# Splitting value products by the contraction, and issuing query turns ahead of stores, in an attention-then-FFN kernel

## Chip, cores, metric

One core of a Trainium2 chip. The metric is device time in microseconds (us), lower is better; it is the span of the profile plus about 2.0 us.

## The reference, cut to what matters

```python
kv  = einsum('bhsd,bhse->bhde', k, v)      # batch 8, 8 heads, 576 rows, 64 columns
out = einsum('bhsd,bhde->bhse', q, kv)
x   = rmsnorm(out) * g_norm                # then (8*576, 512), normed again with rms_g
y   = (silu(x @ w_gate) * (x @ w_val)) @ w_out   # 512 -> 1536 -> 512
```

## The kernel before

TensorE does everything in bfloat16. Batch 0 is the start-up: its x, its weights and its first products are made while the loads arrive. The weights are rounded and scaled by other engines as they land (`round_w`); the contraction of 512 is four slices `s` of 128. First place that the change touches, the products of the first two pairs of hidden blocks on the first half of the tokens, and the turns (transposes by TensorE) of the second half of x:

```python
for blk, s in ((0, 0), (0, 1), (1, 0), (0, 2), (1, 1), (1, 2)):
    round_w(blk, "v", s, GP)                    # GpSimd rounds value weights
# ... gate products of pairs 0 and 1 ...
for blk in range(2):
    round_w(blk, "v", 3, SC)                    # ScalarE rounds the fourth slices
for u in range(2):
    ffn.half_unit(first[1], u, wv_sb, u, 0, 256)       # all four slices of one block
for u in range(2):
    x_turn(Z, u, xs[u], DVE)                           # turn on TensorE, copy on VectorE
for u in range(2):
    ffn.half_unit(second[1], u, wv_sb, 2 + u, 0, 256)
# next: products that need both turned tiles of x
```

Between the two places, batch 1's q is turned as soon as it is loaded and cast:

```python
down_part(0, 2, 4)
turns.q_turn(0, SC)          # first set of eight turns
down_part(1, 2, 4)
turns.q_turn(1, DVE)         # second set
for c in range(2, 4):
    down_part(c, 2, 4)
# then F: the query products of batch 1
```

Second place, the end of batch 0. `down_out` copies an output bank and, after every second one, stores it; `q_rows` lets the transfer engines turn batch 2's queries. Loads, stores and these turns all go through one queue in program order:

```python
alloc_q(2)
cast_q(2, 0, SC)
ffn.down_out(0)
down_part(1, 8, 12)
f_x(0, xs[0], SC); f_x(1, xs[1], SC)       # (two lines in the kernel)
for i in (1, 2, 3):
    cast_q(2, i, SC if i == 1 else DVE)
ffn.down_out(1)                            # first stores
atts = {b: Att(b) for b in range(2, B + 1)}
for c in range(2):
    atts[2].q_rows(c)
# ...
for c in range(2, 4):
    atts[2].q_rows(c)
ffn.down_out(2)
ffn.down_out(3)                            # second stores
```

Of the kernel before, what the change touches and what calls it, by code (L numbers as in the profile page):

```python
# [20 lines left out]
def kernel(  # L21
# [14 lines left out]
    B, H, S, D = q.shape  # L36
# [5 lines left out]
    T = 4  # L42
    MAIN = 128 * T
    TAIL = S - MAIN
    NS = d_model // 128
# [30 lines left out]
    PE, DVE, SC, GP = nc.tensor, nc.vector, nc.scalar, nc.gpsimd  # L76
# [15 lines left out]
    wv_sb = consts.tile([128, NS, d_ff], BF16, name="wv_sb")  # L92
# [47 lines left out]
    def alloc_q(b):  # L140
        bufs[b]["q"] = qb_pool.tile([128, T, H, D], BF16, name="qb")

    def cast_heads(b, h, n, step, engine):

        src = raws[b, "q"].rearrange("p (h t d) -> p t h d", h=H, t=T)
        at = place(h)
        cast(
            engine, bufs[b]["q"][:, :, at : at + (n - 1) * step + 1 : step, :],
            src[:, :, h : h + (n - 1) * step + 1 : step, :],
        )  # L150

    def cast_q(b, i, engine):

        cast_heads(b, i, 2, 4, engine)
# [29 lines left out]
    def round_w(blk, name, s, engine):  # L184
        j0, j1 = W_BLOCKS[blk]
        dst = {"g": wg_sb, "v": wv_sb}[name][:, s, j0 * 128 : j1 * 128]
        src = w_st[name, blk][:, s, :]
        if engine is SC:
            SC.activation(out=dst, in_=src, func=ACT.Copy, scale=rowscale[:, s : s + 1])
        else:  # L190
            engine.tensor_scalar(  # L191
                out=dst, in0=src, scalar1=rowscale[:, s : s + 1], scalar2=1.0, op0=OP.mult, op1=OP.mult
            )
# [49 lines left out]
    xnts = {}  # L243
# [15 lines left out]
    def to_rows(x, n, c, ps, engine):  # L259

        for j in range(NS):
            PE.matmul(  # L262
                ps[:, j, :], lhsT=x[:, 2 * j : 2 * j + 2, :], rhs=identity, is_transpose=True,
                start=(j == 0), stop=(j == NS - 1),
            )
        cast(engine, xnts[n][:, :, 128 * c : 128 * c + 128], ps)
# [198 lines left out]
    class Ffn:  # L465
# [25 lines left out]
        def half_unit(self, ps, u, wt, j, lo, hi):  # L491

            for s in range(NS):
# [2 lines left out]
                    rhs=xnts[self.n][:, s, lo:hi], start=(s == 0), stop=(s == NS - 1),  # L496
                )

        def up_pair(self, i, lo, banks=None):

            banks = banks or self.pair_banks()
            for k, wt in enumerate((wg_sb, wv_sb)):
                for u in range(2):
                    self.half_unit(banks[k], u, wt, 2 * i + u, lo, lo + 256)
            return banks
# [123 lines left out]
    Z = Cols(0, 256, 512, qt0, sqt0, "Z")  # L629
# [44 lines left out]
    def x_turn(cols, c, x, engine, p=att_pool, name="att_ps"):  # L674
        bank = p.tile([128, MAIN], FP32, name=name)
        to_rows(x, cols.n, cols.lo // 128 + c, bank.bitcast(BF16)[:, 0:512].rearrange("p (j t) -> p j t", j=NS), engine)
# [70 lines left out]
    xs = [A.scale(c, oA[c]) for c in range(2)]  # L747
# [4 lines left out]
        x_turn(A, i, xs[i], DVE, *((ops_pool, "o_ps") if i else ()))  # L752
    round_w(1, "g", 2, DVE)
    round_w(1, "g", 3, SC)
    for blk, s in ((0, 0), (0, 1), (1, 0), (0, 2), (1, 1), (1, 2)):
        round_w(blk, "v", s, GP)
    ffn = Ffn(0)
    first, second = ffn.pair_banks(), ffn.pair_banks()
# [12 lines left out]
        round_w(blk, "v", 3, SC)  # L771
    SC.preload_act_table(ACT.Silu)
    xs = [Z.scale(c, oZ[c]) for c in range(2)]
    for u in range(2):
        ffn.half_unit(first[1], u, wv_sb, u, 0, 256)
    for u in range(2):
        x_turn(Z, u, xs[u], DVE)
    for u in range(2):
        ffn.half_unit(second[1], u, wv_sb, 2 + u, 0, 256)
    ffn.gate_pair(0, 0, first)  # L780
    ffn.gate_pair(1, 0, second)
    for name in ("g", "v"):
# [102 lines left out]
    def f_x(c, x, engine):  # L885
        bank = att_pool.tile([128, NS, 128], BF16, name="att_ps")
        to_rows(x, 1, c, bank, engine)
# [3 lines left out]
    def down_part(c, lo, hi):  # L891
        ffn.down_products(c, lo, hi, pools[c])
# [39 lines left out]
    down_part(0, 8, 12)  # L932
    xs = [F.scale(c, F.outa[c]) for c in range(4)]
    alloc_q(2)
    cast_q(2, 0, SC)
    ffn.down_out(0)
    down_part(1, 8, 12)
    f_x(0, xs[0], SC)
    f_x(1, xs[1], SC)
    for i in (1, 2, 3):  # L940
        cast_q(2, i, SC if i == 1 else DVE)
    ffn.down_out(1)
    atts = {b: Att(b) for b in range(2, B + 1)}
    for c in range(2):
        atts[2].q_rows(c)
    down_part(2, 8, 12)
    f_x(2, xs[2], DVE)
    f_x(3, xs[3], DVE)
    down_part(3, 8, 12)
    for c in range(2, 4):  # L950
        atts[2].q_rows(c)
    ffn.down_out(2)
    ffn.down_out(3)



# [28 lines left out]
    for n in range(1, B + 1):  # L985
        ffn = Ffn(n)
# [11 lines left out]
        if n < B:  # L998
# [5 lines left out]
            for i in range(2):  # L1004
                u = o0 + 2 * i
# [9 lines left out]
        b = n + 2  # L1015
# [53 lines left out]
```

## Time and profile before

| | |
|---|---|
| time, first three runs | 319.75 us median (319.25 to 320.18) |
| span of the profiled run | 318.0 us |
| TensorE busy | 97% |
| its wait for GpSimd's rounding, near 20 us | 0.63 us |
| its wait for batch 2's query turns, near 65 us | 0.54 us by the distance of the neighbours' starts |

How to read it: TensorE is the bound, so a change is worth what it takes out of TensorE's idle gaps, and only if no later gate swallows it. The lines are shown in the prediction.

### The profile page before, as it was taken

What the parts mean: (1) busy time and instruction counts of PE and PEld (TensorE: products, weight loads), DVE (VectorE), ACT (ScalarE), POOL (GpSimd) and SP (SyncE); (2) the same over time, 40 slices, a digit from 0 to 9 for tenths busy, and PEclk for the clock granted to TensorE, in tenths of its full rate; (3) what the DMA queues carried; (4) which work ended last, traced back from release to release, by engine and by line L of the source; (5) the groups of instructions that cost most, each with busy time, mean ns of one, the idle gap of its engine ahead of it and who ended that gap; (6) DMA issues with size and microseconds to landing.
All of it is one profiled execution on the core that took longest, in us unless ns stands there. A gap on an engine that the chain in (4) does not pass through costs nothing.

```text
span 318.0 us, 5995 instructions
## 1 busy us (share of the span) xinstructions
PE 308.1 (97%) x2334; PEld 150.3 (47%) x2371; DVE 180.4 (57%) x378; ACT 175.7 (55%) x323; POOL 21.4 (7%) x46
## 2 busy tenths in 40 slices
PE   7899999999999999999999999999999999999995
PEld 3575456444444444444444444444444444444443
DVE  3676768679439922893289427951795079604310
ACT  3577367475657466836683768366745374233321
POOL 1274351100000000000000000000000000000000
PEclk9999999999999999999999999999999999999999
DMA  7999999886379257905790499838002710230014
GB/s 264 361 386 388 376 375 332 136 237 259 75 193 354 77 135 195 364 8 96 195 378 27 89 194 232 316 66 174 28 0 58 142 66 3 56 142 3 0 33 100
DMA packets 60712, 54.95 MB, mean 173 GB/s; under 512 B 36232, under 2 KB 45708, under 8 KB 60684
## 3 DMA queue, kind: packets, MB, share of 16 engines
q1 hardware_dynamic: 60304, 53.92, 57.5%
q10 hardware_dynamic: 380, 0.66, 0.6%
q8 instruction: 18, 0.29, 0.4%
q14 instruction: 10, 0.08, 0.1%
HBM read 37.75 MB, written 9.44 MB: 148 GB/s over the span
## 4 chain that ended last, share of the span: by engine, by line
PE 90%; DMA 5%; SPq 1%; issue 1%; another core or an unknown queue 1%; POOL 1%; ACT 0%; DVE 0%
PE v_ps L477 28%; PE g_ps L477 28%; PE o_ps L519 26%; DMA st<-in_moe_w_val_dram 3%; DMA st<-in_q_dram 2%; PE att_ps L286 2%; PE v_ps L519 1%; PE g_ps L519 1%; PE v_ps L494 1%; DMA out_dram<-o_sb 1%; PE att_ps L326 1%; POOL wv_sb L191 1%; PE o_ps L494 1%; PE att_ps L262 0%
## 5 line engine op out<-in xcount | busy, mean ns | idle before, releaser
L483 DVE TENSOR_TENSOR h_sb<-silu,v_ps 128x512 bf16<-128x512 bf16 x104 | 71.1, 683 | 100.8 <-ACT silu L482 68.1
L477 PE MATMUL v_ps<-xnt,wv_sb 128*128 128x512 bf16 x409 | 106.2, 379 | 0.7
L477 PE MATMUL g_ps<-xnt,wg_sb 128*128 128x512 bf16 x398 | 104.6, 379 | 0.7
L482 ACT ACTIVATE silu<-g_ps 128x512 bf16<-128x512 f32 x104 | 62.1, 597 | 70.7 <-PE g_ps L477 55.0
L519 PE MATMUL o_ps<-wo_sb,h_sb 128*128 128x512 bf16 x386 | 86.8, 379 | 0.4
L477 PEld LDWEIGHTS <-wv_sb 128*128 128x128 bf16 x416 | 40.7, 98 | 49.1
L519 PEld LDWEIGHTS <-h_sb 128*128 128x128 bf16 x420 | 40.6, 98 | 47.7 <-issue 0.4
L477 PEld LDWEIGHTS <-wg_sb 128*128 128x128 bf16 x416 | 39.6, 98 | 46.4
L104 ACT COPY o_sb<-o_ps 128x512 f32<-128x512 f32 (+1 forms) x34 | 19.7, 579 | 40.2 <-PE o_ps L519 36.6
L373 DVE TENSOR_TENSOR xna<-outa,s1y 128x512 bf16<-128x512 bf16 x28 | 17.9, 684 | 0.0
L104 ACT CAST vb<-st 128x576 bf16<-128x576 f32 x25 | 15.7, 673 | 3.7 <-DMA st<-in_v_dram 3.7
L104 ACT CAST qb<-st 128x512 bf16<-128x512 f32 (+1 forms) x30 | 16.3, 602 | 2.1 <-DMA st<-in_q_dram 2.1
L356 DVE TENSOR_REDUCE ssq<-sq 128x16 f32<-128x1024 bf16 x14 | 17.1, 1220 | 0.5
L356 DVE TENSOR_REDUCE ssq<-sqt 128x16 f32<-128x1024 bf16 x14 | 17.1, 1220 | 0.5
L104 ACT CAST kb<-st 128x576 bf16<-128x576 f32 x20 | 12.4, 674 | 0.0
L341 ACT ACTIVATE sq<-att_ps 128x512 bf16<-128x512 f32 x14 | 7.6, 594 | 4.3 <-PE att_ps L326 3.6
L619 PE MATMUL att_ps<-kv_all 128*128 128x512 bf16 (+1 forms) x21 | 7.6, 489 | 1.2 <-DVE sel L608 1.2
L355 DVE TENSOR_TENSOR sq<-sq,gsq 128x512 bf16<-128x512 bf16 x14 | 5.9, 421 | 4.9 <-ACT sq L341 4.9
L106 DVE CAST kb<-st 128x576 bf16<-128x576 f32 x12 | 5.9, 508 | 4.0 <-DMA st<-in_k_dram 4.0
L106 POOL CAST wo_sb<-st 128x512 bf16<-128x512 f32 x12 | 7.2, 632 | 7.4 <-DMA st<-in_moe_w_out_dram 7.4
L341 ACT ACTIVATE sqt<-o_ps 128x512 bf16<-128x512 f32 x14 | 7.6, 598 | 0.0
L347 ACT CAST outa<-att_ps 128x512 bf16<-128x512 f32 x14 | 7.5, 594 | 0.0
(148 smaller groups left out, 180.6 us busy)
## 6 DMA issues: line engine op xcount, KB each, us to landing
st<-in_k_dram SPq DMA_DIRECT2D x7, 1152.0 KB, 10.8
st<-in_v_dram SPq DMA_DIRECT2D x7, 1152.0 KB, 12.6
out_dram<-o_sb SPq DMA_DIRECT2D x14, 512.0 KB, 3.1
st<-in_q_dram SPq DMA_DIRECT2D x6, 1024.0 KB, 8.0
st<-in_moe_w_out_dram SPq DMA_DIRECT2D x6, 512.0 KB, 10.4
st<-in_moe_w_gate_dram SPq DMA_DIRECT2D x4, 512.0 KB, 10.6
st<-in_moe_w_val_dram SPq DMA_DIRECT2D x4, 512.0 KB, 9.9
st<-in_k_dram SPq DMA_DIRECT2D x4, 288.0 KB, 4.4
```

The lines of the kernel that those rows point to most:

```text
L104: engine.copy(out=dst, in_=src)
L106: engine.tensor_copy(out=dst, in_=src)
L286: PE.matmul(self.kv_ps[x][to, a, :], lhsT=kb[rows, 2 * a + x, c, :], rhs=vb[rows, 2 * a + x, c, :], start=(a == 0 and c == 0), stop=(a == ...
L341: SC.activation(out=self.in_place(self.sq[i][:, 0], g), in_=bank, func=ACT.Square)
L347: SC.copy(out=self.in_place(rows, g), in_=bank)
L356: DVE.reduce_sum(out=self.ssq[:, c], in_=sq, axis=AX.X)
L373: DVE.tensor_tensor(out=self.xna[c], in0=self.outa[c], in1=self.alpha[:, c, :].to_broadcast([128, H, D]), op=OP.mult)
L477: PE.matmul(ps, lhsT=wt[:, s, j * 128 : (j + 1) * 128], rhs=x[:, s, :], start=(s == 0), stop=(s == NS - 1),)
L482: SC.activation(out=silu, in_=g_ps, func=ACT.Silu)
L483: DVE.tensor_tensor(out=self.h[:, j, :], in0=silu, in1=v_ps, op=OP.mult)
L519: PE.matmul(self.o_ps[c], lhsT=self.h[:, j, c * 128 : (c + 1) * 128], rhs=wo_sb[:, j, :], start=(j == 0), stop=(j == NF - 1),)
L619: PE.matmul(ps[:, 0:w], lhsT=warm_sb[:, 0:128], rhs=warm_sb[:, 0:w], start=True, stop=True, skip_group_check=True)
```

## The change

Its intent: fill the wait for rounding with slices that are ready and with the turns of x; and issue the queries' turns before the stores, so that they land before TensorE wants them. No work is added or removed. Two stretches are cut where they are marked.

```diff
+        def half_units(self, ps, wt, j, lo, ss):
+            for u in range(2):
+                for s in ss:
+                    PE.matmul(
+                        ps[:, u, :], lhsT=wt[:, s, (j + u) * 128 : (j + u + 1) * 128],
+                        rhs=xnts[self.n][:, s, lo : lo + 256],
+                        start=(u == 0 and s == 0), stop=(u == 1 and s == NS - 1), skip_group_check=True,
+                    )
@@ part 1 @@
-    for blk, s in ((0, 0), (0, 1), (1, 0), (0, 2), (1, 1), (1, 2)):
+    for blk, s in ((0, 0), (0, 1), (1, 0), (1, 1), (0, 2), (1, 2)):
         round_w(blk, "v", s, GP)
... cut ...
-    for u in range(2):
-        ffn.half_unit(first[1], u, wv_sb, u, 0, 256)
-    for u in range(2):
-        x_turn(Z, u, xs[u], DVE)
-    for u in range(2):
-        ffn.half_unit(second[1], u, wv_sb, 2 + u, 0, 256)
+    ffn.half_units(first[1], wv_sb, 0, 0, (0, 1))
+    ffn.half_units(second[1], wv_sb, 2, 0, (0, 1))
+    x_turn(Z, 0, xs[0], DVE)
+    ffn.half_units(first[1], wv_sb, 0, 0, (2, 3))
+    x_turn(Z, 1, xs[1], DVE)
+    ffn.half_units(second[1], wv_sb, 2, 0, (2, 3))
@@ part 2 @@
-    cast_q(2, 0, SC)
-    ffn.down_out(0)
+    for i in range(T):
+        cast_q(2, i, SC if i < 2 else DVE)
+    atts = {b: Att(b) for b in range(2, B + 1)}
+    for c in range(T):
+        atts[2].q_rows(c)
     down_part(1, 8, 12)
     f_x(0, xs[0], SC)
     f_x(1, xs[1], SC)
... cut: the old casts, turns and stores between and behind the other parts go ...
     down_part(3, 8, 12)
-    for c in range(2, 4):
-        atts[2].q_rows(c)
-    ffn.down_out(2)
-    ffn.down_out(3)
+    for c in range(T):
+        ffn.down_out(c)
```

More of the change, by code (lines that the diff above doesn't have):

```diff
@@ L939 @@
     f_x(1, xs[1], SC)
-    for i in (1, 2, 3):
-        cast_q(2, i, SC if i == 1 else DVE)
-    ffn.down_out(1)
-    atts = {b: Att(b) for b in range(2, B + 1)}
-    for c in range(2):
-        atts[2].q_rows(c)
     down_part(2, 8, 12)
@@ L949 @@
     down_part(3, 8, 12)
-    for c in range(2, 4):
-        atts[2].q_rows(c)
-    ffn.down_out(2)
-    ffn.down_out(3)
+    for c in range(T):
+        ffn.down_out(c)
     def load_q_tails():
```

## The prediction

> **What bounds the kernel now.** I read the page first, then the list of TensorE's waits, then the timeline around each wait, because the change moves only a few dozen instructions and its worth is decided by individual gaps.
>
> ```profile
> PE 308.1 (97%) x2334; PEld 150.3 (47%) x2371; DVE 180.4 (57%) x378; ACT 175.7 (55%) x323; POOL 21.4 (7%) x46
> ```
>
> TensorE is busy 97% of a 318.0 us span, the others at most 57%. No work of TensorE is removed, so only its idle gaps can be won. From TensorE's list of waits, the two that the change is aimed at (us in total, times, longest):
>
> ```profile
> PE v_ps L494 <- POOL wv_sb L191: 0.6, 1, 0.6
> PE o_ps L326 <- DMA qt<-qb: 0.4, 1, 0.4
> ```
>
> The first: the value products of the first pair stand at the third slice of the contraction, because GpSimd has not rounded that slice of the weights yet. TensorE's timeline there (start, duration), then GpSimd's:
>
> ```profile
> 20.50 0.83 PE L494 MATMUL v_ps<-xnt,wv_sb 128*128 128x256 bf16 x6 [0.63 <-POOL wv_sb L191]
> 21.16 0.61 PE L262 MATMUL att_ps<-identity,xna 128*128 128x128 bf16 x8
> 21.61 1.04 PE L494 MATMUL v_ps<-xnt,wv_sb 128*128 128x256 bf16 x8
> 22.48 1.04 PE L494 MATMUL o_ps<-xnt,wg_sb 128*128 128x256 bf16 x8
> ```
> ```profile
> 18.60 2.75 POOL L191 TENSOR_SCALAR wv_sb<-st,rowscale 128x256 bf16<-128x256 f32 x6 [1.00 <-DMA st<-in_moe_w_val_dram]
> ```
>
> A 256-column matmul costs (22.48 - 21.61)/8 = 0.109 us start to start, a turn (21.61 - 21.16)/8 = 0.056 us, a rounding 2.75/6 = 0.46 us. The wait ends at 20.50, just after the fourth rounding (18.60 + 4 x 0.46 = 20.44).
>
> The second gap is larger than the list says. TensorE from the value products of a unit to those of the next, with batch 2's query products between them, and below it the same place one batch later:
>
> ```profile
> 63.73 1.03 PE L477 MATMUL v_ps<-xnt,wv_sb 128*128 128x512 bf16 x4
> ...
> 66.67 1.03 PE L477 MATMUL v_ps<-xnt,wv_sb 128*128 128x512 bf16 x4
> ```
> ```profile
> 93.39 1.03 PE L477 MATMUL v_ps<-xnt,wv_sb 128*128 128x512 bf16 x4
> ...
> 95.79 1.03 PE L477 MATMUL v_ps<-xnt,wv_sb 128*128 128x512 bf16 x4
> ```
>
> Same work: 2.94 us against 2.40, so this wait costs 0.54 us. Its cause is the order of the transfer queue:
>
> ```profile
> 55.04 1.26 SPq L539 DMA_DIRECT2D out_dram<-o_sb  x2
> 56.40 6.10 SPq L300 DMA_TRANSPOSE qt<-qb  x4
> 62.61 1.92 SPq L539 DMA_DIRECT2D out_dram<-o_sb  x2
> ```
>
> The four query turns stand behind the first two stores. The first is issued at 56.40, the last at 61.2 with up to 4.3 us to landing (all four: 2.5 to 4.3), near 65.5, when the query products resume (65.58).
>
> Between the two gaps lies a third place, which the change doesn't touch: batch 1's second half of q. VectorE casts it when the load lands, and TensorE turns it:
>
> ```profile
> 42.40 0.63 DVE L106 CAST qb<-st 128x512 bf16<-128x512 f32 x2 [0.72 <-DMA st<-in_q_dram]
> ```
> ```profile
> 42.79 0.83 PE L833 MATMUL g_ps<-identity,qb 128*128 128x128 bf16 x8
> 43.67 0.38 PE L519 MATMUL o_ps<-wo_sb,h_sb 128*128 128x512 bf16 x1
> 43.88 0.61 PE L833 MATMUL v_ps<-identity,qb 128*128 128x128 bf16 x8
> 44.33 0.59 PE L519 MATMUL g_ps<-wo_sb,h_sb 128*128 128x512 bf16 x2
> ```
>
> The second set of eight turns takes 44.33 - 43.88 = 0.45 us. Two 512-column matmuls precede it at 0.216 each (a row shows one; a record is missing), so the first set took 43.88 - 0.43 - 42.79 = 0.66. TensorE already stood about 0.2 us for the cast, which ended at 43.03. The page's row of transfer engines (DMA) is at 9 tenths in every slice from 8 us to 56 us: this load arrives when the transfer engines get to it.
>
> **What the Trainium skill says.** "PSUM — Partial Sum Buffer", section Engine vs sequencer instructions: matmuls start and complete in program order. The trace agrees: during the 0.63 us nothing behind the waiting product ran, though the rounded slice for the second pair could have been next. The same page, section The four PSUM rules: the first-flag clears the bits of the whole bank, and a later group's first matmul without it overwrites. The new value products set it once per bank, on the first column half, so their sums should be right; no run before shows it. "Perfetto Trace Analysis", section Tensor Engine Instruction: a matmul's end is estimated from its size, so I use starts alone; the trace agrees (rows of 0.38 us start 0.216 apart). "DMA: Bandwidth & Descriptors", section Queues, rings and completion order: within a queue each transfer engine consumes descriptors in order. The page puts 60304 of 60712 packets on one queue, so turns and stores share it.
>
> **Part 1: value products by halves.** Nothing is added or removed: 16 products of 256 columns, 8 turns, 6 roundings; GpSimd's fourth and fifth roundings change places. By the costs above:
> - Gate products end at 19.24. First pair, slices 0 and 1: slice 1 is rounded at 19.52, its product starts at 19.68, the four are done near 20.00.
> - Second pair, slices 0 and 1: roundings 3 and 4, ready at 19.98 and 20.44. The first product goes at 20.1, the others from 20.50: done at 20.50 + 3 x 0.109 = 20.83.
> - Turn of x, first tile, 4 x 0.056: 21.05 (its scaling is long done). First pair, slices 2 and 3 (rounding 5 at 20.90): 21.49. Second turn: 21.71. Second pair (rounding 6 at 21.35): 22.15 instead of 22.48, a gain of 0.33.
> - But the next products need the second tile's copy. Before, the copies started at 21.59 and lasted 0.75 for two; a turn's copy starts about 0.2 us after its last matmul issues. Now the second starts near 21.91, takes 0.41 and lets TensorE go at about 22.4. So 0.1 us is left, 0.33 at most.
> - From there to 42.79 TensorE runs without a listed wait, so it arrives at the turns of q 0.1 to 0.3 us early, and the cast is still at 43.03, as the transfers before it don't change. The early arrival is spent waiting. Part 1 on the end: 0.
>
> **Part 2: queries ahead of the stores.** The turns need all four casts. VectorE's two end at 54.21 and do not move; ScalarE's second moves from 53.90 to about 52.0, into the 0.36 us that ScalarE stands before its copies at 52.94 plus the place of the store's copy. The turns start at about 54.3 instead of 56.40, 2.1 us earlier. They last 6.1 us of issue: the last is issued near 59.1 and, with the slow 4.3, lands at 63.4. The products that need it come at 65.1. Slack 1.7 us, so the wait should vanish whole: 0.54 us. ScalarE's four copies of the outputs come in one row behind, 54.0 to about 56.0, ending as before (55.37 + 0.62), with the first activation of the next block at 56.27; the last two keep their times, and they are the ones whose banks the next units need. The stores land some microseconds later, and nothing waits for them. After this TensorE has no listed wait to the end, so the gain should stay.
>
> Sum: 0 + 0.54. 319.75 - 0.54 = **319.2 us**.
>
> **Rivals.**
> 1. Part 1 is not absorbed: if q's landing is paced by buffers that TensorE frees, the end gains another 0.1 to 0.3 (318.9 to 319.1). For it: a load is issued only when its staging buffer is free. Against: the full DMA row.
> 2. The turns gain nothing: batch 2's values land late (GpSimd starts on them at 56.84 after 7.79 us idle), so a turn issued at 54.3 queues behind them on some transfer engines. If all begin only at 56.8 they end near 63, still in time. If instead they delay the values: those casts have some 2 us of slack on GpSimd and VectorE before the states at 60.42. Should it run out, one wait replaces another: 319.75 or up to 1 us more.
> 3. The next block starts late, as the output copies stand in a row on ScalarE: at most one copy, 0.6 us, cancelling the gain (319.8). Against: both orders end at the same copy.
>
> **Range and chances.** The three runs before span 0.93 us, more than the expected gain; a median of three can move by 0.4. The rivals add -0.3 to +0.6. I take 318.5 to 320.0. A verdict of faster or slower at 2% needs 6.4 us; all TensorE waits listed sum to 4 us. So 0.01 faster, 0.98 within, 0.01 slower.
>
> **What would show it.** Right: the wait on the query turns is gone and the span between the two value products near 64 to 66 is 2.40 us; turns issued near 54.3; the wait for GpSimd shorter, products behind the turns of x at about 22.4; the first set of q turns longer than 0.66 us by what was won there, and the second set's start within 0.1 us of 43.88. Wrong: that start clearly earlier than 43.8 (rival 1), a new wait of TensorE near 60 or 55, or a wait still near 65.

## The result, and the profile after

The changed kernel took 318.87 us in the median of six runs (318.69 to 319.73), the kernel before 319.96 (319.15 to 320.39) beside it. The ratio is 0.9977, 95% interval 0.9957 to 0.9997: the same within 2%. A ratio here is the mean time of one kernel's fast runs over that of the other's of the same rounds, so it is not quite the ratio of the medians. In a second session the changed kernel gave 0.9995. The profiled run of the changed kernel has a span of 317.6 us, 0.4 us less than before, and computes the right result.

From the changed kernel's page, and the end of TensorE's list of waits (the wait for the query turns is not in it any more, and that for GpSimd is 0.2 instead of 0.6 us):

```profile
PE 308.5 (97%) x2334; PEld 150.3 (47%) x2371; DVE 181.3 (57%) x378; ACT 175.6 (55%) x323; POOL 21.5 (7%) x46
```
```profile
PE g_ps L398 <- ACT qt L104: 0.2, 1, 0.2
PE v_ps L503 <- POOL wv_sb L191: 0.2, 1, 0.2
```

Part 1 in TensorE's timeline after (start, duration; the rest as before), and GpSimd's roundings below it:

```profile
20.53 0.50 PE L503 MATMUL v_ps<-xnt,wv_sb 128*128 128x256 bf16 x3 [0.17 <-POOL wv_sb L191]
20.87 0.39 PE L262 MATMUL att_ps<-identity,xna 128*128 128x128 bf16 x4
21.09 0.60 PE L503 MATMUL v_ps<-xnt,wv_sb 128*128 128x256 bf16 x4
21.53 0.39 PE L262 MATMUL att_ps<-identity,xna 128*128 128x128 bf16 x4
21.75 0.60 PE L503 MATMUL v_ps<-xnt,wv_sb 128*128 128x256 bf16 x4
22.43 1.03 PE L494 MATMUL o_ps<-xnt,wg_sb 128*128 128x256 bf16 x8
```
```profile
18.63 2.76 POOL L191 TENSOR_SCALAR wv_sb<-st,rowscale 128x256 bf16<-128x256 f32 x6 [0.74 <-DMA st<-in_moe_w_val_dram]
```

The value products are done at 21.75 + 4 x 0.109 = 22.19, but the next ones start at 22.43: they wait for VectorE's copy of the second tile, which runs from 21.95 to 22.37. From GpSimd's first rounding to them it is 22.43 - 18.63 = 3.80 us; before it was 22.48 - 18.60 = 3.88. So part 1 wins 0.08 us at this point.

At the turns of batch 1's q, VectorE's casts and TensorE after:

```profile
42.51 0.63 DVE L106 CAST qb<-st 128x512 bf16<-128x512 f32 x2 [0.81 <-DMA st<-in_q_dram]
```
```profile
42.73 0.99 PE L843 MATMUL g_ps<-identity,qb 128*128 128x128 bf16 x8
43.78 0.38 PE L529 MATMUL o_ps<-wo_sb,h_sb 128*128 128x512 bf16 x1
43.99 0.61 PE L843 MATMUL v_ps<-identity,qb 128*128 128x128 bf16 x8
```

TensorE came 0.06 us earlier than before (42.73 against 42.79); the load landed 0.11 later (42.51 against 42.40), and the second set of turns is 0.11 later (43.99 against 43.88). The start follows the load, not TensorE's arrival.

Part 2: the transfer queue, and TensorE's value products on both sides of batch 2's query products:

```profile
54.47 5.23 SPq L300 DMA_TRANSPOSE qt<-qb  x4
59.81 3.09 SPq L549 DMA_DIRECT2D out_dram<-o_sb  x4
```
```profile
63.83 1.03 PE L477 MATMUL v_ps<-xnt,wv_sb 128*128 128x512 bf16 x4
...
66.24 1.03 PE L477 MATMUL v_ps<-xnt,wv_sb 128*128 128x512 bf16 x4
```

The turns start at 54.47, and the distance is 2.41 us, as in every later batch, instead of 2.94. One thing doesn't fit: each of the four turns now lands 2.5 us after its issue, while before the last took 4.3. Had the last turn of the kernel before taken 2.5 us as well (61.2 + 2.5 = 63.7), it would have been in time for the products at 65.1, and there would have been no wait to remove. So the order of the queue alone cannot have made it.

The packets of the transfers in the kernel before tell what else was there. The list, put together from the trace's packet records, is of packets that took over 0.4 us between 60 and 66 us, start in us, duration in us, kind, bytes (on this queue 256 bytes are the turns' packets, 4 bytes the signals of landing, 2048 bytes those of the stores behind them):

```
63.08 0.932 instruction 16384
63.10 1.698 hardware_dynamic 256
63.11 1.701 hardware_dynamic 256
63.13 1.674 hardware_dynamic 256
... (11 more of 1.46 to 1.64 us, of 256 and of 4 bytes; then 8 of 0.97 to 1.11 us, of 2048 bytes)
```

A packet of 256 bytes of a turn takes 0.018 us in the median. Here those that were moving when 16384 bytes of instructions were fetched took up to 1.7 us. I take this fetch to be TensorE's: its queue holds 18 in the whole run, for 4728 recorded TensorE instructions, one per some 260. "Runtime: NRT & Kernel Launch", section Instruction fetch mechanics, of the Trainium skill says that engines stream their program in blocks of 16 KiB, that is 256 instructions, which agrees. In the changed kernel the fetch comes at 63.71, when the turns' last packet has been down since 60.45.

Two theories follow. *Queue order*: the turns are late because they stand behind the stores. *Collision*: the last turn is late in those executions in which it meets a fetch of instructions late enough; the order only decides whether the turns are still moving at that time.

### The profile page after: what moved, and what is told of

It reads as the page before. It is cut to its first block, busy times and chain, and to the rows that moved or that the text cites. A ratio compares the mean times of both kernels' runs of the same rounds, so it can differ in the third digit from the quotient of the medians.

```text
span 317.6 us, 5996 instructions
## 1 busy us (share of the span) xinstructions
PE 308.5 (97%) x2334; PEld 150.3 (47%) x2371; DVE 181.3 (57%) x378; ACT 175.6 (55%) x323; POOL 21.5 (7%) x46
## 4 chain that ended last, share of the span: by engine, by line
PE 90%; DMA 5%; SPq 1%; another core or an unknown queue 1%; issue 1%; POOL 1%; DVE 0%; ACT 0%
PE v_ps L477 28%; PE g_ps L477 28%; PE o_ps L529 26%; DMA st<-in_moe_w_val_dram 3%; DMA st<-in_q_dram 2%; PE att_ps L286 2%; PE v_ps L529 1%; PE g_ps L529 1%; DMA out_dram<-o_sb 1%; PE att_ps L326 1%; PE o_ps L494 1%; POOL wv_sb L191 1%; PE o_ps L326 0%; PE att_ps L262 0%
## 5 line engine op out<-in xcount | busy, mean ns | idle before, releaser
L347 ACT CAST outa<-o_ps 128x512 bf16<-128x512 f32 x14 | 7.5, 591 | 0.0
```

The lines of the kernel that those rows point to most:

```text
L347: SC.copy(out=self.in_place(rows, g), in_=bank)
```

## The experiments

All outputs are right. "Distance" is from the value products before batch 2's query products to those behind them.

### Each part alone

Edit: the diff above, one part at a time.

> Part 1 alone (value products by halves), queues as before. Prediction's theory: absorbed at the turns of batch 1's q; ratio to before 0.999 to 1.001; first products behind the turns of x about 0.05 to 0.1 us earlier relative to the gate products than in the kernel before (4.1 us from the second gate products' start to them becomes 4.0), the second set of q turns starts within 0.1 us of 1.5 us after the cast of q, as before; 2.94 us between the two value products near 64 to 66 stays. Rival (not absorbed): ratio 0.9985 or lower and the q turns earlier by 0.2 us or more.

Part 1 alone: 319.89 us median of six (319.44 to 321.14), ratio 1.0001 (0.9980 to 1.0021). From the first rounding to the products behind the turns of x 3.80 us, as in the changed kernel. The second set of q turns at 43.75, its last cast at 42.61. The distance was 2.77 us, not 2.94: the fetch was at 62.26 this time.

> Part 2 alone (queries ahead of the stores). Theory: the whole of the gain; ratio 0.9983 give or take 0.001 (0.54 us of 320), 2.40 us between the two value products, no wait for the query turns. Rival (the two parts share the gain): ratio 0.9992 or higher, with a wait left.

Part 2 alone: 319.67 us (319.26 to 319.98), ratio 0.9991 (0.9974 to 1.0008). Distance 2.41 us, no wait. So by the traces part 2 makes the whole effect on the end, but the times are too coarse to tell 0.9983 from 0.9992. The trace of part 1 already shows that the wait of the old queue order is not of fixed length.

### The kernel before, again

No edit.

> The kernel before once more as its own control. Ratio 1.000 give or take 0.001, which says how finely the others may be read. Its single times should again fall in two groups, near 319.2 and near 320.1. New trace: if the queue order alone makes the wait on the query turns, it is 2.94 us between the two value products again; if it is the last turn meeting a fetch of TensorE's instructions (in the first trace at 63.08 us, with turn packets of 256 bytes lasting 1.7 us instead of 0.018), then the length varies with where that fetch falls, and is 2.40 us where it misses the turn.

320.29 us (319.52 to 320.74), ratio to its own other runs 1.0008 (0.9989 to 1.0026). Its transfer queue, and TensorE around batch 2's query products:

```profile
55.05 1.26 SPq L539 DMA_DIRECT2D out_dram<-o_sb  x2
56.42 7.25 SPq L300 DMA_TRANSPOSE qt<-qb  x4
63.77 1.19 SPq L539 DMA_DIRECT2D out_dram<-o_sb  x2
```
```profile
63.76 1.03 PE L477 MATMUL v_ps<-xnt,wv_sb 128*128 128x512 bf16 x4
...
66.16 1.03 PE L477 MATMUL v_ps<-xnt,wv_sb 128*128 128x512 bf16 x4
```

The same program, the same order, turns issued at the same time (56.42): distance 2.40 us and no wait at all. The fetch came at 61.89, the turn's packets took up to 0.9 us, and the last was down at 64.08 instead of 64.83. This rules out queue order as the sufficient cause: the 0.54 us belong to one execution. Of three traces of the old order, the fetch at 61.89, 62.26 and 63.08 us gave 0, 0.37 and 0.54 us of wait. The two groups of times that had been expected cannot be seen in its six runs.

### Moving the fetch

First try, an edit that takes four warm-up products, eight instructions, out:

```diff
     A.alloc_sums()
-    warm(A.bank, 1)
...
-    warm(A.bank, 1)
...
-    warm(banksZ[0], 2)
```

> The kernel before, queue order untouched, less four warm-up matmuls near 12 to 15 us (eight TensorE instructions fewer, so the same instruction fetch comes about eight instructions, some 0.8 us, later, after the last query turn has moved its data). Theory queue order: the last turn lands as late as before, 2.94 us between the two value products. Rival, collision with the fetch: last turn lands 2.5 us after issue instead of 4.3, and 2.40 us between the value products, though the stores still go first.

The trial missed its aim: the fetch near 53 us came 1 us later (54.05), but that near 62 was at 61.98, no later than in the kernel before. The last packet was down at 64.10, distance 2.41 us, no wait; 319.71 us (319.47 to 320.33), ratio 0.9998 (0.9973 to 1.0022). It agrees with the trace before, and tells nothing more. What sets the fetch's moment within a microsecond stays open.

Second try: batch 0's later products in two column halves, which adds 176 instructions at almost the same time, queue order untouched.

```diff
-            for ps, wt in ((g_ps, wg_sb), (v_ps, wv_sb)):
-                for s in range(NS):
-                    PE.matmul(ps, lhsT=..., rhs=x[:, s, :], ...)
+            halves = ((0, 256), (256, MAIN)) if self.n == 0 else ((0, MAIN),)
+            for ps, wt in ((g_ps, wg_sb), (v_ps, wv_sb)):
+                for lo, hi in halves:
+                    for s in range(NS):
+                        PE.matmul(ps[:, lo:hi], lhsT=..., rhs=x[:, s, lo:hi], ...)
# and the same for the down products up to the sixth block
```

> The kernel before, queue order untouched, with batch 0's later products cut into two column halves: 176 TensorE instructions more ahead of 60 us at nearly the same time, so the instruction fetch that came at 61.9 to 63.1 us comes about 176 instructions earlier, near 58 to 59 us, and the next one not before 63.6. Collision theory: the last query turn's packets stay short, it lands 2.5 us after issue, no wait of TensorE, 2.40 us between the value products though the stores go first. Queue-order theory: a wait of 0.4 to 0.5 us as in the first trace.

319.0 us in one run of unknown state. The fetches fell at 55.66 and 69.28: further from 58 than I had reckoned, but both clear of the turns. There are 19 fetches in the run instead of 18, which fits 176 more TensorE instructions. Its queue:

```profile
54.50 1.25 SPq L543 DMA_DIRECT2D out_dram<-o_sb  x2
55.86 6.01 SPq L300 DMA_TRANSPOSE qt<-qb  x4
61.97 1.19 SPq L543 DMA_DIRECT2D out_dram<-o_sb  x2
```

```profile
63.19 1.03 PE L479 MATMUL v_ps<-xnt,wv_sb 128*128 128x512 bf16 x4
...
65.59 1.03 PE L479 MATMUL v_ps<-xnt,wv_sb 128*128 128x512 bf16 x4
```

The turns still stand behind the first stores. No packet of the turns took over 0.25 us, the last, issued at 60.6, was down at 62.62, and the distance was 2.40 us (63.19 to 65.59). With the fetch away the long packets of the late turns are away and the last turn is down 2.0 us after its issue (60.6 to 62.62), where the first trace had 3.6 (61.2 to 64.83). It is one execution, but the fetch was moved on purpose, so the collision rests on more than coincidence.

The other traces agree. In all five in which packets of the late turns overlap a fetch, these packets end 0.79 to 0.81 us after the fetch ends, wherever it ends:

| trace | fetch, start to end | end of the turns' long packets | wait |
|---|---|---|---|
| before again | 61.89 to 63.25 | 64.04 to 64.06 | 0 |
| less warm-up products | 61.98 to 63.28 | 64.06 to 64.08 | 0 |
| part 1 alone | 62.26 to 63.73 | 64.51 to 64.53 | 0.37 |
| before | 63.08 to 64.01 | 64.80 to 64.82 | 0.54 |
| stores first (below) | 62.76 to 63.90 | 64.69 to 64.71 | 1.04 |

So in the four traces of the old order the end of the fetch tells when the last turn is down, and with it the wait. How a fetch holds these packets, and why for 0.8 us after its own end, no run shows. A fetch is also not the only thing that makes packets long: in every trace, this one included, some at the start of the second turn take 0.25 to 0.82 us, over 1.5 us after the last fetch. These never reached the last turn, and their cause is open.

### More of the old order, and less

All four stores ahead of the turns:

```diff
-    for c in range(2):
-        atts[2].q_rows(c)
     down_part(2, 8, 12)
...
-    for c in range(2, 4):
-        atts[2].q_rows(c)
     ffn.down_out(2)
     ffn.down_out(3)
+    for c in range(T):
+        atts[2].q_rows(c)
```

> The kernel before with all four stores ahead of the four query turns (the opposite of part 2): turns issued from about 57.7 instead of 56.4, the last near 62.5. Queue order alone (each turn lands 2.5 us after issue): last landing 65.0, so a wait of 0 to 0.4 us, 2.4 to 2.8 us between the value products. With an instruction fetch falling between 62 and 65 us on top, the last turns' packets last over 0.9 us and the distance is 2.9 to 4 us. Ratio 1.000 to 1.004.

321.19 us (320.74 to 321.64), ratio 1.0049 (1.0030 to 1.0068): the one result that the times show clear of noise as slower than the kernel before, by half a per cent, still within the 2%, and more than the 1.004 that had been allowed for. TensorE:

```profile
65.56 0.29 PE L326 MATMUL o_ps<-kv_all,qt 64*128 64x64 bf16 x8 [0.25 <-DMA qt<-qb]
66.28 0.29 PE L326 MATMUL o_ps<-kv_all,qt 64*128 64x64 bf16 x8 [0.43 <-DMA qt<-qb]
```

The turns were issued from 58.41, later than the 57.7 expected, the last at 63.23, and a fetch at 62.76 stretched packets of the turns to 0.9 us. Distance 3.45 us, so a wait of 1.04. By an estimate, the order would matter here even without the fetch: 63.23 + 2.5 = 65.7 is 0.4 us past the need, which is near 65.3 in this execution (65.1 and the 0.2 us by which Q, defined below, is later). Order and collision then add up; the old order left 65.1 - 63.7 = 1.4 us of slack, which only a late collision used up.

Only the turns ahead of the first store, nothing else of part 2:

```diff
+    atts = {b: Att(b) for b in range(2, B + 1)}
+    for c in range(T):
+        atts[2].q_rows(c)
     ffn.down_out(1)
-    atts = {b: Att(b) for b in range(2, B + 1)}
-    for c in range(2):
-        atts[2].q_rows(c)
# (the later two turns are taken out too)
```

> The kernel before with nothing but the four turns issued ahead of the first store; order on TensorE, VectorE and ScalarE unchanged. Turns from about 54.7 us, 0.3 us later than in the changed kernel (they wait for ScalarE's second cast), last landing near 61.2: no wait, 2.40 us between the value products whatever the fetch does. If ScalarE's regrouping mattered, a wait stays. Ratio 0.999 give or take 0.001.

319.27 us (318.70 to 319.43), ratio 0.9986 (0.9967 to 1.0005). Distance 2.41 us, no wait, though the second turn had packets of 0.55 us (no fetch was near). So part 2 is this move; by the trace the regrouping of ScalarE's copies adds nothing.

### The changed kernel, again

No edit.

> The changed kernel once more. No wait at the query products wherever the fetch falls, 2.40 us. The first result (ratio 0.9977) was larger than the 0.54 us can give; if the wait is there in only part of the executions of the kernel before, the true mean gain is 0.2 to 0.4 us and this ratio is nearer 0.999 (0.9975 to 1.0005).

319.58 us (318.62 to 319.91), ratio 0.9995 (0.9977 to 1.0013). Distance 2.41 us. All seven traces with the turns ahead of the stores, this one and the others, have 2.41. But in none of them did a fetch fall among the turns: their last packet was down 2.1 to 3.3 us before the next fetch. So "wherever the fetch falls" is not tested.

The traces add up in an unexpectedly simple way. "Q" is the start of the second set of q turns, "V" that of the value products behind batch 2's query products; all in us:

| trace | Q | V - Q | wait in it | span |
|---|---|---|---|---|
| before | 43.88 | 22.79 | 0.54 | 318.0 |
| before again | 43.90 | 22.26 | 0 | 317.5 |
| part 1 alone | 43.75 | 22.63 | 0.37 | 317.9 |
| part 2 alone | 43.82 | 22.25 | 0 | 317.4 |
| changed | 43.99 | 22.25 | 0 | 317.6 |
| changed again | 43.02 | 22.24 | 0 | 316.6 |
| turns before the first store | 43.07 | 22.25 | 0 | 316.7 |
| stores first | 44.08 | 23.30 | 1.04 | 318.7 |

From V to the end of the span it is 251.3 to 251.5 us in each. So a span is Q + 22.25 + the wait + 251.4. Q, which the landing of q sets, varies by 1.06 us; the wait varies by 0.54 in the old order. The two traces with an early q were early long before: GpSimd's first rounding of value weights starts at 17.70 and 17.75 us in them, at 18.00 to 18.77 in the other six. So, in these two at least, the whole start-up with its loads was early, not this load alone. In the first session the changed kernel's spans were 316.7 to 316.9 in four runs and 317.6 to 317.7 in two, which are the spans that the two traces of it have with an early and a late q. The larger part of the scatter in the times is thus in no part of the change.

### Opening the gate at the turns of q

One pair of down products more ahead of the turns, in the changed kernel:

```diff
     down_part(0, 2, 4)
-    turns.q_turn(0, SC)
     down_part(1, 2, 4)
+    turns.q_turn(0, SC)
     turns.q_turn(1, DVE)
```

> The changed kernel with the turns of batch 1's q behind one more pair of down products (0.43 us of work moved into the wait for q). If q's landing absorbs what part 1 wins, the stall there (0.1 to 0.4 us in the traces so far) now falls: the sixteen turns take 0.9 us in a row, the products behind them start 0.2 to 0.4 us earlier after the cast of q, ratio to before 0.9975 to 0.9990. If the turns' copies were the bound instead, the products of the next stage start no earlier and the ratio is that of the changed kernel.

319.77 us (319.31 to 320.21), ratio 1.0006 (0.9989 to 1.0023): no gain in the times, where 0.9975 to 0.9990 had been expected, which is a miss. The trace has what was expected: the sixteen turns in 0.9 us from 43.35, and the query products of batch 1 2.33 us after the last cast of q starts, against 2.63 in the changed kernel. But q landed late in that execution (last cast at 42.96, the latest of all). The gain of 0.30 us behind the cast is there by the trace; in the times it is not shown.

Then q loaded ahead of half a megabyte of the output weights, and turned ahead of the products that need those:

```diff
     load_kv(1, "v", nc.sync)
-    load_wo(0, (2,))
     load_q(1)
+    load_wo(0, (2,))
...
-    down_part(0, 2, 4)
     turns.q_turn(0, SC)
-    down_part(1, 2, 4)
     turns.q_turn(1, DVE)
-    for c in range(2, 4):
-        down_part(c, 2, 4)
+    for j in (2, 3):
+        for c in range(4):
+            down_part(c, j, j + 1)
```

> The changed kernel with batch 1's q loaded ahead of the half megabyte of the output weights that stood before it, and with its turns ahead of the down products that need those weights: the gate at the turns of q is opened by 1.3 us. Theory (q's landing is what absorbs part 1): the turns no longer wait, and the products behind the down products start some 0.4 us earlier (22.9 us after the first products behind the turns of x, where the changed kernel had 23.05). Ratio 0.9965 to 0.9990. Rival: the output weights, now later, are the new gate and the gain is under 0.2 us.

319.31 us (318.25 to 320.71), ratio 0.9981 (0.9956 to 1.0007). VectorE casts all of q in one row, done before TensorE comes for it:

```profile
40.05 1.16 DVE L106 CAST qb<-st 128x512 bf16<-128x512 f32 x4
```

From batch 1's states to its query products it is 3.47 us (40.62 to 44.10) against 3.90 in the changed kernel (41.58 to 45.48), with no wait at the turns. From the products behind the turns of x it is 22.63 us, where 22.9 had been expected.

> The same with part 1 undone (part 2 and q first). If the gate is open, part 1's own gain, 0.05 to 0.1 us at the products behind the turns of x, now reaches the end, so this kernel is that much slower than the one with part 1 from the gate products to the query products of batch 1; if the new gate is the output weights, both are equal there.

319.20 us (318.52 to 320.03), ratio 0.9978 (0.9955 to 1.0001). Measured from GpSimd's first rounding of value weights, which neither part can move, to batch 1's query products: 26.43 us with part 1 (17.67 to 44.10), 26.48 without (19.32 to 45.80). With the gate open, part 1's 0.09 us is 0.05 further on; the rest may go to the output weights, now rounded just as TensorE wants them. A twentieth of a microsecond between two traces is as far as this can be read. The two variants are the shortest by their traces; by the times no version is shown to beat the changed kernel.

## Why the prediction was right, point by point

- **The number.** 319.2 us was predicted, 318.87 measured, within 318.5 to 320.0. Part of the closeness is luck: the two medians differ by 1.09 us, twice what the traces explain, since four of the six runs of the changed kernel had, by their spans, an early q, and the interval of the ratio reaches from 0.1 to 1.4 us.
- **Part 1 at the turns of x.** Predicted: products done near 22.15, copy from 21.91, next products near 22.4, 0.1 us left. Measured: 22.19, 21.95, 22.43 and 0.08. Over all traces, from the first rounding to those products it is 3.88 to 3.89 us in the eight without part 1, 3.79 to 3.80 in the five with it. The bound by the second tile's copy, not by TensorE's products, was the step that made 0.33 us into 0.1.
- **Its absorption at q.** Right. In the nine traces with the gate in place and the program around it as it was, TensorE started the first set of turns between 0.57 us before and 0.19 us after the start of the last cast of q, and the second set always started 1.14 us after the start of that cast. What TensorE wins upstream it waits there. The sign set for it, a second set within 0.1 us of 43.88, was just missed (43.99): the load came 0.11 us later.
- **Part 2's size and issue.** Turns from 54.47 where 54.3 was predicted; the wait gone; distance 2.41 where 2.40 was. The slack was some 4.3 us, not 1.7: the four issues took 5.23 us, not 6.1, and the last turn, issued at 58.43 instead of 59.1, took 2.5 us to land, not 4.3. It was down at 60.9, and the need is near 65.2.
- **Part 2's cause.** The step "Its cause is the order of the transfer queue" was incomplete, and with it the reading of 0.54 us as a property of the kernel. Shown in its place: in that order the wait needs a fetch of TensorE's instructions that meets the last turn late enough; it was 0, 0.37 and 0.54 us in three traces of that order, a mean of 0.3 (0.2 with the trace less warm-up products). The four ratios of kernels with the turns ahead and nothing else of weight (0.9977, 0.9991, 0.9986, 0.9995) average 0.9987, or 0.4 us (0.9988 with the three that move the turns of q as well): of that size, though each interval is wider than the effect. Issuing the turns first removes the wait all the same, because they are down before that fetch comes; that the slack would also cover a collision is an estimate.
- **Rivals.** None came about: the second set did not start earlier than the load allowed, no wait near 55 or 60 us appeared, and the first activation of the next block started at 56.37, behind the last copy.

## What to carry to other kernels

Before a gap counts as a property of a kernel, take the unchanged kernel's trace a second time: a wait can belong to one execution, and the same program may show it or not. Follow time won upstream to the next thing that arrives by itself, such as a load; if the start behind it stands at a fixed distance from the landing, the win ends there. An early issue can be worth having as slack (here some 4.3 us, by the estimate above) even where the wait that it removes was chance.

## What the Trainium skill lacked or had wrong

- "DMA: Bandwidth & Descriptors", sections DMA Transpose (X-bar) and Rules for kernel authors: they treat turns beside other turns and say that a transpose next to ordinary DMAs needs nothing, which is about correctness and held here. The section Queues, rings and completion order tells how queues share the transfer engines, but that a fetch of instructions can be one of the parties, and what it costs a turn, stands nowhere that I looked: packets of 256 bytes took up to 1.7 us instead of 0.018 while 16384 bytes of instructions came in, and the turn landed after 4.3 us instead of 2.5.
- "Runtime: NRT & Kernel Launch", section Instruction fetch mechanics: it calls the cost of a block boundary mostly hidden. No wait of TensorE for instructions is listed here, but through the turn the fetch cost it up to 0.54 us in the kernel before.
- No page that I looked up has the scatter of loads from execution to execution: batch 1's q let TensorE go on between 43.02 and 44.08 us in the traces of the table; among those without a wait that makes up the spread of the spans, 316.6 to 317.6 us.
